# Attention with mixed heads and two MLP blocks: products with v spread over the next chunk, single banks for mixed scores, reciprocals on POOL, token weights made inside attention

## The chip, the core and the metric

The kernel runs on one core of one Trainium2 chip. The metric is the device time of one execution in microseconds. Engines: PE (TensorE: matmuls, and PEld for loading weights), DVE (VectorE), ACT (ScalarE), POOL (GpSimd) and SP, which here only issues transfers. Each engine works through its own instructions in the order in which they were written; semaphores make one wait for another.

## What is computed

```python
scores = scale * np.matmul(q, k.transpose(0, 1, 3, 2))        # B 2, H 12, S 448, D 64
scores = np.einsum('bhij,hg->bgij', scores, w_pre)            # heads are mixed
scores = scores - np.max(scores, axis=-1, keepdims=True)
attn = np.exp(scores)
attn = attn / (np.sum(attn, axis=-1, keepdims=True) + 1e-09)
attn = np.einsum('bhij,hg->bgij', attn, w_post)               # and mixed again
out = np.matmul(attn, v)
...
h = np.maximum(xt @ w_tok1, 0.0) @ w_tok2                     # token MLP over the 448 tokens
u = x + h.transpose(0, 2, 1)
h2 = np.maximum(u @ w_ch1, 0.0) @ w_ch2                       # channel MLP
return (u + h2)
...                                                           # then a gated block, GELU and a layer norm
```

The weights of the MLPs arrive as 64-bit floats and are turned into pairs of 32-bit parts (h and l) on the chip.

## The kernel before, in words

**Chunks and steps.** For each of the two batches the 448 rows of queries are cut into four chunks of 120, 120, 120 and 88 rows. A chunk is worked in steps of 20 rows; the last chunk has five, the fifth of them half as large. That makes 46 steps, numbered 0 to 45 here; chunks begin at steps 0, 6, 12, 18, 23, 29, 35 and 41.

**One step** goes through these names. `qk` (L317) makes the scores of two heads for a whole chunk on PE, into the one pair of banks `psA`, and a copy to SBUF follows (`S`, L319, on ACT; a chunk has six of these). Transfers issued by SP (L346, `P<-S`, two a step, 210 KB each) lay the scores out with the heads along the partitions, in a ring of eight tiles. `pre` (L354, PE) mixes the heads, into a pair of banks of `psB`, of which there are two. `nm` (L360, DVE) is the negative maximum, `E` (L365, ACT, two instructions) the exponential with its sum `sm`. `rc` and `rr` (L371, L373, DVE) make the reciprocal, `wt` (L377, POOL) scales the mixing weights with it. `post` (L398, PE, 64 small matmuls) mixes the heads again into the one pair of banks `psC`, and `AT` (L406, a copy on DVE, after the last `qk` on ACT) turns the result for the product with v.

**The product with v** (`av`, L421 and L427, 96 matmuls for a chunk) stands in one block behind the first step of the next chunk. It uses `psA`, the banks of `qk`. Its result is copied to `xT` by DVE and then by ACT (L433, L437).

**The order** is the order of the code: a loop over steps i, in which `pre`, `nm` and `E` work two steps ahead (LP = 2), `rc`, `rr` and `wt` one step ahead, and the transfers five steps ahead (LD = 5). Two `qk` can fall into one step. The last `qk` is in step 36.

**Behind step 36** the weights of the token MLP (four pieces, `p_t1`, `p_t2`) are fetched and converted: per piece one ACT instruction (L102), four on DVE (L120 to L126), a copy on ACT and a subtraction on DVE or POOL. `pump(4)` takes four such stages a step. In the last two steps the first batch of `xT` is turned by PE (`xps`, L446) and split (`xh` on ACT, `xl` on DVE). Then comes the last product with v, and with `t1ps` the token MLP begins; from there on the matmuls follow each other to the end.

## Time and profile before

| | us |
|---|---|
| three runs, median | 546.38 |
| three runs, lowest and highest | 544.72, 547.17 |
| the profiled execution | 544.84 |
| its span | 543.06 |
| PE busy in it | 498.2 (92%) |
| DVE busy | 353.4 (65%) |
| ACT busy | 240.8 (44%) |
| POOL busy | 157.7 (29%) |

The span runs from the first to the last instruction; 1.78 us of the execution lie outside it. A busy PE is not a PE at its peak, since matmuls overlap and their ends are modelled. In the profile two kinds of rows matter here: the chain of waits (the work that ended last, followed back from the end: start, duration, engine, tile, line) and the busy time of each engine in chosen stretches, with the granted clock of PE.

### The profile page before, as it was taken

The numbers are of one execution on the slowest core, as the hardware profiler recorded it, in microseconds if no ns is written. First come the engines' busy times: TensorE is split into PE (matmuls) and PEld (weight loads), VectorE is DVE, ScalarE is ACT, GpSimd is POOL, SyncE is SP. The second block draws the span as 40 slices with busy tenths as digits, with TensorE's granted clock in tenths as the row PEclk, the third lists the DMA queues.
The fourth block names the chain that finished last, engine by engine and source line by source line (L and its number), as shares of the span: only waits on it lengthen the run. The fifth ranks groups of instructions, "written<-read, shape, count | busy, mean of one in ns | idle before, by whom it ended". The sixth has DMA issues, their size and how long they took to land.

```text
span 543.1 us, 14017 instructions
## 1 busy us (share of the span) xinstructions
PE 498.2 (92%) x5998; PEld 408.4 (75%) x5998; DVE 353.4 (65%) x536; ACT 240.8 (44%) x454; POOL 157.7 (29%) x193
## 2 busy tenths in 40 slices
PE   7888989898897665899999999999999999999997
PEld 4345565664664553899999999999999998888986
DVE  2654657466474456295455768778887984897972
ACT  3453747467375644355333444333332344454320
POOL 2011111111021121028222322344544454057500
PEclk9989999999999775899999999999999999999999
DMA  4588435537252632031032433343353333102222
GB/s 164 178 227 233 144 95 168 156 109 212 96 179 100 183 115 64 1 118 58 1 116 98 152 120 116 113 157 100 123 168 98 100 106 123 40 1 68 88 103 102
DMA packets 25699, 63.71 MB, mean 117 GB/s; under 512 B 2836, under 2 KB 18756, under 8 KB 25636
## 3 DMA queue, kind: packets, MB, share of 16 engines
q1 hardware_dynamic: 25348, 62.42, 37.0%
q8 instruction: 47, 0.77, 0.6%
q10 hardware_dynamic: 288, 0.39, 0.2%
q14 instruction: 16, 0.13, 0.1%
HBM read 40.70 MB, written 2.75 MB: 80 GB/s over the span
## 4 chain that ended last, share of the span: by engine, by line
PE 79%; ACT 7%; DVE 6%; DMA 6%; issue 2%; SPq 0%; POOLq 0%; POOL 0%; ACTq 0%; DVEq 0%
PE post L398 6%; PE av L421 6%; PE c2ps L574 5%; PE c1ps L574 5%; PE c1ps L572 5%; PE c2ps L572 5%; PE c1ps L573 5%; PE c2ps L573 5%; PE qk L317 5%; DMA P<-S 3%; PE pre L354 3%; ACT E L365 2%; PE ups L573 2%; PE ups L572 2%; PE ups L574 2%
## 5 line engine op out<-in xcount | busy, mean ns | idle before, releaser
L147 POOL TENSOR_TENSOR wl<-cv,wh 128x768 fp32r<-128x768 f32 x28 | 52.6, 1877 | 138.8 <-ACT wh L146 104.6
L398 PEld LDWEIGHTS post<-wt,E 60*64 60x64 f32 x2880 | 54.9, 141 | 37.3 <-issue 26.8
L377 POOL TENSOR_SCALAR wt<-wd_post,rr 128x60 f32<-128x60 f32 x90 | 28.5, 332 | 168.1 <-DVE rr L373 119.6
L398 PE MATMUL post<-wt,E 60*64 60x60 f32 (+1 forms) x2880 | 55.8, 224 | 13.8 <-ACT AT L406 9.7
L365 ACT ACTIVATE E<-pre,nm 128x448 f32<-128x448 f32 x90 | 56.5, 635 | 24.8 <-DVE rc L371 18.0
L360 DVE TENSOR_REDUCE nm<-pre 128x2 f32<-128x896 f32 (+1 forms) x46 | 48.9, 1063 | 23.3 <-PE pre L354 23.3
L317 PE MATMUL qk<-kn,qn 64*64 64x448 f32 x384 | 48.3, 563 | 11.9 <-ACT xT L433 4.8
L354 PE MATMUL pre<-P,wp 64*64 64x448 f32 (+1 forms) x360 | 53.5, 557 | 5.6 <-DMA P<-S 4.1
L124 DVE SCALAR_TENSOR_TENSOR cv<-raw,cv 128x768 uint32<-128x768 uint32 (+3 forms) x44 | 54.2, 1231 | 1.4
L319 ACT COPY S<-qk 128x896 f32<-128x896 f32 x42 | 38.1, 907 | 35.4 <-PE qk L317 32.5
L574 PE MATMUL c2ps<-r1h,wl 128*128 128x448 f32 x144 | 52.6, 365 | 0.0
L573 PE MATMUL c1ps<-ul,wh 128*128 128x448 f32 x144 | 52.6, 365 | 0.0
L574 PE MATMUL c1ps<-uh,wl 128*128 128x448 f32 x144 | 52.6, 365 | 0.0
L572 PE MATMUL c2ps<-r1h,wh 128*128 128x448 f32 x144 | 52.6, 365 | 0.0
L573 PE MATMUL c2ps<-r1l,wh 128*128 128x448 f32 x144 | 52.6, 365 | 0.0
L572 PE MATMUL c1ps<-uh,wh 128*128 128x448 f32 x144 | 52.6, 365 | 0.0
L406 DVE COPY AT<-post 128x840 f32<-128x840 f32 (+1 forms) x37 | 38.9, 1052 | 16.3 <-PE post L398 15.4
L102 ACT ACTIVATE cv<-raw 128x768 f32<-128x768 f32 (+3 forms) x44 | 36.2, 824 | 23.5 <-POOL wl L147 16.7
L126 DVE SCALAR_TENSOR_TENSOR cv<-raw,cv 128x768 uint32<-128x768 uint32 (+3 forms) x44 | 40.2, 914 | 1.1
L317 PEld LDWEIGHTS qk<-kn,qn 64*64 64x64 f32 x384 | 13.8, 135 | 35.7 <-ACT S L319 14.1
L146 ACT CAST wh<-cv 128x768 fp32r<-128x768 f32 x28 | 23.4, 836 | 32.7 <-DVE cv L126 32.0
L120 DVE TENSOR_SCALAR cv<-cv 128x768 f32<-128x768 f32 (+3 forms) x44 | 30.7, 698 | 9.1 <-ACT cv L102 8.9
(188 smaller groups left out, 988.5 us busy)
## 6 DMA issues: line engine op xcount, KB each, us to landing
P<-S SPq DMA_DIRECT2D x88, 210.0 KB
raw<-in_w_ch_dram SPq DMA_DIRECT2D x24, 768.0 KB
raw<-in_w_v_dram SPq DMA_DIRECT2D x6, 512.0 KB
raw<-in_w_u_dram SPq DMA_DIRECT2D x4, 768.0 KB
raw<-in_w_out_dram SPq DMA_DIRECT2D x6, 512.0 KB
qn<-in_q_dram SPq DMA_DIRECT2D x14, 192.0 KB
vn<-in_v_dram SPq DMA_DIRECT2D x6, 448.0 KB
out_dram<-xT SPq DMA_DIRECT2D x12, 224.0 KB
```

Of the source, the lines that this page charges most:

```text
L124: nc.vector.scalar_tensor_tensor(fi, lo, 29, fi, op0=ALU.logical_shift_right, op1=ALU.bitwise_or)
L126: nc.vector.scalar_tensor_tensor(fi, hi, 0xC0000000, fi, op0=ALU.bitwise_and, op1=ALU.bitwise_or)
L147: nc.gpsimd.tensor_tensor(dst[1], f, f32(dst[0]), op=ALU.subtract)
L317: nc.tensor.matmul(ps[cols, j, :S], lhsT=qn[b, c, i // QG][rows, i % QG, h], rhs=KX[b, i][rows], start=True, stop=True)
L354: nc.tensor.matmul(ps[cols, e, :S], lhsT=wp[rs], rhs=ring[(2 * i + r) % NP_BUFS][rs], start=True, stop=True)
L360: nc.vector.tensor_reduce(out=nm[:, :ne], in_=ps[:, :ne, :S], axis=AX.X, op=ALU.max, negate=True)
L365: nc.scalar.activation(t, ps[:, e, :S], AF.Exp, bias=nm[:, e:e + 1], scale=1.0, accum_out=sm[:, e:e + 1])
L398: nc.tensor.matmul(ps[cols, r, o:o + w.stop - w.start], lhsT=E[rs, t * 64:(t + 1) * 64], rhs=wt[rs, w], start=True, stop=True)
L406: copy(dst.rearrange("p g (a i) -> p a g i", i=HB), src.rearrange("p a (g i) -> p a g i", i=HB))
L572: nc.tensor.matmul(ps, lhsT=lh, rhs=rh, start=(start and i == 0), stop=False)
L573: nc.tensor.matmul(ps, lhsT=lh, rhs=rl, start=False, stop=False)
L574: nc.tensor.matmul(ps, lhsT=ll, rhs=rh, start=False, stop=(stop and i == n - 1))
```

## The change

The change touches the attention part and the way in which the token weights are made. In words:

- The product with v of a chunk is cut into four parts (heads 0 and 1 of six pairs, 2, 3 and 4, 5), which stand in different steps of the next chunk, in a bank of their own (`psV`), each with one copy to `xT` on DVE. The last chunk's product is in two parts behind the loop, in banks of `psB`.
- `psB` becomes three single banks instead of two pairs. `nm` becomes two instructions of 448 columns instead of one of 896.
- `rc` and `rr` go from DVE to POOL, the reciprocal as a power of minus one.
- `qk` stands ahead of `pre` and at most one falls into a step, but for one step; `E` stands behind `post`; `AT` stays on DVE to step 43.
- The pieces of the token weights are fetched from step 2 on, and one stage is taken per step from step 4 to step 36, with the first operation on POOL instead of DVE; behind step 38 the first channel piece follows at one stage a step instead of four.
- The transposes of the first batch stand in steps 42 to 45, two a step.
- At the start, the mixing weights are loaded ahead of the second chunk's q, `wp` is scaled behind the first six `qk`, and the twelve first `qk` go through two pairs of banks instead of three. The first q tiles of chunk 1 are loaded twice.
- `v` of the second batch is loaded three steps later.

```diff
-        if i in p_t1:
-            nc.scalar.copy(dst[0], f)
-            yield
-            nc.vector.tensor_tensor(dst[1], f, f32(dst[0]), op=ALU.subtract)
-        elif scale is None:
-            nc.scalar.copy(dst[0], f)
+        if scale is None:
+            nc.scalar.copy(dst[0], f)
+            if early(i):
+                yield
             nc.gpsimd.tensor_tensor(dst[1], f, f32(dst[0]), op=ALU.subtract)
...
-            nc.vector.tensor_scalar(f, f, MIN_HI, MAX_HI, op0=ALU.max, op1=ALU.min)
+            (nc.gpsimd if early(i) else nc.vector).tensor_scalar(f, f, MIN_HI, MAX_HI, op0=ALU.max, op1=ALU.min)
...
-    psB = actx.enter_context(tc.tile_pool(name="psB", bufs=2, space=PSUM))
+    psB = actx.enter_context(tc.tile_pool(name="psB", bufs=3, space=PSUM))
+    psV = actx.enter_context(tc.tile_pool(name="psV", bufs=1, space=PSUM))
...
+    def b_max(i):
+        ne = steps[i][3]
+        st[i]["nm"] = ap_.tile([P, 2], F32, tag="nm", name=f"nm{i}", bufs=3)
+        for e in range(ne):
+            nc.vector.tensor_reduce(out=st[i]["nm"][:, e:e + 1], in_=st[i]["pre"][e][:, :S], axis=AX.X, op=ALU.max,
+                                    negate=True)
...
-        nc.vector.tensor_scalar(rc[:, :ne], st[i]["sm"][:, :ne], 1e-9, None, op0=ALU.add)
+        nc.gpsimd.tensor_scalar(rc[:, :ne], st[i]["sm"][:, :ne], 1e-9, None, op0=ALU.add)
         rr = ap_.tile([P, 2], F32, tag="rr", name=f"rr{i}", bufs=3)
-        nc.vector.reciprocal(rr[:, :ne], rc[:, :ne])
+        nc.gpsimd.tensor_tensor(rr[:, :ne], rc[:, :ne], mone[:, :ne], op=ALU.pow)
...
+    load_const()
     for g in range(NQ):
         load_q(0, 1, g)
-    load_const()
...
-    scale_pre()
-    both = ((psA, "A"), (psB, "B"), (psB, "B"))
+    both = ((psA, "A"), (psC, "C"))
...
+        if x == 0:
+            add(at[-1], scale_pre)
...
+        elif x + 1 < NCH:
+            for g in range(NQ):
+                add(at[0] + g, load_q, *chunks[x + 1], g)
...
-        add(first[1, 0] + 1 + g, load_v, 1, g)
+        add(first[1, 0] + 4 + g, load_v, 1, g)
...
+    add(2, w_dma)
...
+    AVS = ((0, 1), (2,), (3, 4), (5,))
+    todo = []
+    for x in range(NCH - 1):
+        f0, f1 = first[chunks[x + 1]], first[chunks[x + 2]] if x + 2 < NCH else NB
+        for hps in AVS:
+            todo.append((f0 + hps[0] * (f1 - f0) // NP, *chunks[x], hps))
+
+    def next_av(i):
+        while todo and todo[0][0] <= i:
+            _, b, c, hps = todo.pop(0)
+            av(b, c, hps, nc.vector.tensor_copy)
+
+    def next_turn(i, n):
+        if i + LD > NB and turns:
+            ps = one(psV, "V", f"xps0_{len(turns)}") if n else pair(psA, "A", f"xps0_{len(turns)}")[:, 0]
+            turn(ps, *turns.pop(0))
...
     for i in range(-LD, NB):
         for fn, a in extra.get(i, []):
             fn(*a)
-        if 0 <= i + LP < NB:
+        ahead = 0 <= i + LP < NB
+        due = list(scores.get(i, []))
+        if due:
+            qk(*due.pop(0))
+        if ahead:
             b_pre(i + LP)
-        due = scores.get(i, [])
-        if due:
-            qk(*due[0])
-        if 0 <= i + LP < NB:
-            b_exp(i + LP)
+        next_turn(i, 0)
+        if ahead:
+            b_max(i + LP)
         if 0 <= i + 1 < NB:
             b_norm(i + 1)
+        for d in due:
+            qk(*d)
         if i >= 0:
+            next_av(i)
             b_post(i)
-            for d in due[1:]:
-                qk(*d)
-            b_turn(i, nc.vector.tensor_copy if i <= LAST else nc.scalar.copy)
-            if i in starts and i:
-                av(*chunks[chunks.index(steps[i][:2]) - 1])
+        if ahead:
+            b_exp(i + LP)
+        if i >= 0:
+            b_turn(i, nc.vector.tensor_copy if ahead else nc.scalar.copy)
+        next_turn(i, 1)
         if i + LD < NB:
             b_dma(i + LD)
...
-        if i > LAST + 2:
-            pump(4)
+        if 4 <= i <= LAST or i > LAST + 2:
+            pump(1)
...
-    av(*chunks[-1])
+    for x, copy in enumerate((nc.vector.tensor_copy, nc.scalar.copy)):
+        hps = range(x * (NP // 2), (x + 1) * (NP // 2))
+        av(*chunks[-1], hps, copy, (psB, "B"))
```

PE around the product with v of chunk 1 (`av_1`), before: steps 12 and 13 (`post` ends step 12).

```order
L398 MATMUL post_1101<-wt_0_1034,E_0_964 64x60 x12
L398 MATMUL post_1101<-wt_0_1034,E_0_964 64x30 x4
L398 MATMUL post_1101<-wt_1_1036,E_1_966 64x60 x12
L398 MATMUL post_1101<-wt_1_1036,E_1_966 64x30 x4
L421 MATMUL av_1_1135<-AT_1_663,vn_0_316 64x120 x12
L421 MATMUL av_1_1135<-AT_1_663,vn_1_374 64x120 x12
L421 MATMUL av_1_1135<-AT_1_663,vn_2_447 64x120 x12
L427 MATMUL av_1_1135<-AT_1_663,vn_0_316 64x120 x4
L427 MATMUL av_1_1135<-AT_1_663,vn_1_374 64x120 x4
L427 MATMUL av_1_1135<-AT_1_663,vn_2_447 64x120 x4
L354 MATMUL pre_1188<-P_100,wp 64x448 x2
L354 MATMUL pre_1188<-P_101,wp 64x448 x2
```

PE in the changed kernel, step 15 of the same chunk, with two of the six pairs of heads of chunk 1.

```order
L329 MATMUL qk_0_2_1365<-kn_1_599,qn_0_0_819 64x448 x4
L370 MATMUL pre_0_1371<-P_101,wp 64x448
L370 MATMUL pre_1_1372<-P_101,wp 64x448
L370 MATMUL pre_0_1371<-P_102,wp 64x448
L370 MATMUL pre_1_1372<-P_102,wp 64x448
L443 MATMUL av_1_3_1388<-AT_1_709,vn_1_394 64x120 x6
L443 MATMUL av_1_3_1388<-AT_1_709,vn_2_465 64x120 x6
L449 MATMUL av_1_3_1388<-AT_1_709,vn_0_332 64x120 x2
L449 MATMUL av_1_3_1388<-AT_1_709,vn_1_394 64x120 x2
L419 MATMUL post_1406<-wt_0_1301,E_0_1271 64x60 x12
L419 MATMUL post_1406<-wt_0_1301,E_0_1271 64x30 x4
```

The block of 96 matmuls has become four groups of 32 or 16, each between `pre` and `post` of a step, and `qk` has moved ahead of `pre`.

ACT behind the last `qk` before, steps 37 to 39: `E` and `AT` take turns, and from step 39 the conversion of weights (L102) follows.

```order
L365 ACTIVATE E_0_2907,sm_2906<-pre_2899,nm_2904 128x448
L365 ACTIVATE E_1_2909,sm_2906<-pre_2899,nm_2904 128x448
L406 COPY AT_2_2742<-post_2919 128x4x42x5
L365 ACTIVATE E_0_2965,sm_2964<-pre_2957,nm_2962 128x448
L365 ACTIVATE E_1_2967,sm_2964<-pre_2957,nm_2962 128x448
L406 COPY AT_2_2742<-post_2977 128x4x42x5
L365 ACTIVATE E_0_3023,sm_3022<-pre_3015,nm_3020 128x448
L365 ACTIVATE E_1_3025,sm_3022<-pre_3015,nm_3020 128x448
L406 COPY AT_2_2742<-post_3035 128x4x42x5
L102 ACTIVATE cv_3073<-raw_2955 112x512
```

DVE in the changed kernel in steps 37 and 38: `AT` stands here, behind the two `nm` and the copy of a part of the product with v.

```order
L376 TENSOR_REDUCE nm_3022<-pre_0_3016 128x1
L376 TENSOR_REDUCE nm_3022<-pre_1_3017 128x1
L456 COPY xT<-av_1_2_3033 128x12x10
L427 COPY AT_2_2906<-post_3043 128x4x42x5
L376 TENSOR_REDUCE nm_3092<-pre_0_3086 128x1
L376 TENSOR_REDUCE nm_3092<-pre_1_3087 128x1
L456 COPY xT<-av_1_3_3103 128x2x12x10
L427 COPY AT_2_2906<-post_3121 128x4x42x5
```

In these steps ACT has kept only `E`, and `AT` has moved to DVE; the first operation on the token weights, which followed in step 39, is not among them.

## Rows read from the trace of the kernel before

**Rows 1.** Busy time by stretch: us, then each engine (instructions), granted clock, DMA share, GB/s.

```profile
0.00:25.33 25.33, 20.46 (x202) 9.39 (x204) 10.39 (x15) 9.56 (x16) 4.12 (x14) 1.00 0.52 170
25.33:56.55 31.22, 26.74 (x649) 16.80 (x647) 17.27 (x30) 15.05 (x36) 4.81 (x16) 0.95 0.78 216
56.55:169.03 112.48, 101.16 (x2776) 66.87 (x2777) 70.33 (x123) 66.20 (x152) 17.60 (x59) 1.00 0.45 139
169.03:224.66 55.63, 35.33 (x812) 27.27 (x805) 28.46 (x56) 27.71 (x60) 8.15 (x17) 0.72 0.38 113
224.66:543.06 318.40, 314.49 (x1566) 288.09 (x1566) 226.99 (x313) 122.26 (x195) 123.00 (x87) 1.00 0.30 97
```

**Rows 2.** Chain of waits, steps without product with v: start, us, what.

```profile
153.30 0.78 PE pre L354 x8
154.08 0.75 PE qk L317 x8
154.83 0.91 PE post L398 x64
```

**Rows 3.** Chain of waits at a product with v, and the turning copy of step 36.

```profile
160.74 3.84 PE av L421 x72
164.58 0.82 PE av L427 x24
165.42 0.80 DVE xT L433
166.24 0.79 ACT xT L433
...
169.03 1.07 DVE AT L406
```

**Rows 4.** Chain of waits in a step with two score products.

```profile
150.56 0.81 ACT S L319
151.41 0.98 PE qk L317 x8
```

**Rows 5.** Chain of waits behind step 36.

```profile
181.15 1.00 DVE nm L360
182.24 1.34 ACT E L365 x4
183.58 0.90 ACT AT L406
184.61 1.93 PE post L398 x64
...
208.85 0.57 DVE xl L450
```

**Rows 6.** Busy time by stretch, two short ones, columns as in the first group.

```profile
132.00:136.00 4.00, 2.54 (x70) 1.34 (x62) 2.36 (x4) 2.15 (x5) 0.60 (x2) 1.00 0.67 225
180.00:184.00 4.00, 1.28 (x27) 0.37 (x19) 2.94 (x6) 1.76 (x5) 0.89 (x2) 0.91 0.83 213
```

**Rows 7.** DVE by line and shape: count, busy us, mean ns, idle before.

```profile
L406 DVE COPY AT<-post 128x840 f32<-128x840 f32 x36 | 38.3, 1065 | 16.3 <-PE post L398 15.4
L433 DVE COPY xT<-av 128x360 f32<-128x360 f32 x6 | 4.7, 791 | 22.0 <-PE av L427 22.0
L124 DVE SCALAR_TENSOR_TENSOR cv<-raw,cv 128x768 uint32<-128x768 uint32 x28 | 40.2, 1435 | 0.9
```

**Rows 8.** Instructions of one tile, ns as least/median/most: two of POOL.

```profile
L377 POOL TENSOR_SCALAR wt<-wd_post,rr x90: 310/317/907, 23.7 to 204.0; 128x60 f32<-128x60 f32 x90
L748 POOL TENSOR_TENSOR rq<-rs,mhalf x7: 549/552/562, 473.5 to 492.3; 128x1 f32<-128x1 f32 x7
```

**Rows 9.** Timeline: the start's scaling, a maximum of one bank, a slow conversion.

```profile
9.05 0.20 DVE L70 TENSOR_SCALAR wp<-wd_pre 128x64 f32<-128x64 f32 x1 [8.05 <-DMA wd_pre<-in_w_pre_dram]
105.40 0.62 DVE L360 TENSOR_REDUCE nm<-pre 128x1 f32<-128x448 f32 x1 [0.78 <-PE pre L354]
203.00 1.25 DVE L122 TENSOR_SCALAR cv<-cv 128x448 uint32<-128x448 uint32 x1
```

More of the change, by code (lines that the diff above doesn't have):

```diff
@@ L126, in w_conv @@
             nc.vector.scalar_tensor_tensor(fi, hi, 0xC0000000, fi, op0=ALU.bitwise_and, op1=ALU.bitwise_or)
-            w_abs(i + 1)
+            if not early(i):
+                w_abs(i + 1)
         yield
-        if p_t2[0] <= i <= p_c1[1]:
+        if i in p_c1[:2]:
             yield
@@ L153, in conv_steps @@
         for i in range(len(pieces)):
+            while i not in wstate["raw"]:
+                yield
             for _ in w_conv(i):
@@ L158, in conv_steps @@
             yield
+            if early(i + 1):
+                yield
     def pump(n):
@@ L346, in b_dma, with one @@
             nc.sync.dma_start(out=ring[(2 * i + r) % NP_BUFS][PAD:PAD + ne * HW], in_=src)
+    def one(pool, tag, nm):
+        return pool.tile([P, 512], F32, tag=tag, name=nm)
     def b_pre(i):
         ne = steps[i][3]
-        ps = st[i]["pre"] = pair(psB, "B", f"pre{i}")
+        ps = st[i]["pre"] = [one(psB, "B", f"pre{i}_{e}") for e in range(ne)]
         for r, cols in enumerate(HALVES):
@@ L407, in b_turn, with av @@
         st[i] = None
-    def av(b, c):
+    def av(b, c, hps, copy, pool=None):
         s0, n = CH[c]
@@ L413, in av @@
         cols = IB * (nb + (rest > 0))
-        ps = pair(psA, "A", f"av{b}_{c}")
+        ps = one(*(pool or (psV, "V")), f"av{b}_{c}_{hps[0]}")
         at = AT[b, c]
-        for hp in range(NP):
-            x, o = hp % 2, hp // 2 * cols
+        for m, hp in enumerate(hps):
+            o = slice(m * cols, (m + 1) * cols)
             for s in range(NK // 2):
                 for j, out_rows in enumerate(HALVES):
-                    w = vn[b, hp // 2][:, ((x * 2 + j) * (NK // 2) + s) * D:][:, :D]
-                    nc.tensor.matmul(ps[out_rows, x, o:o + cols], lhsT=w,
-                                     rhs=at[:, s * H + x * (H // 2) + hp // 2 * 2 + j, :cols],
-                                     start=(s == 0 and hp < 2), stop=False, skip_group_check=True)
@@ L424, in av @@
-        for hp in range(NP):
-            x, o = hp % 2, hp // 2 * cols
+                    w = vn[b, hp // 2][:, ((hp % 2 * 2 + j) * (NK // 2) + s) * D:][:, :D]
+                    nc.tensor.matmul(ps[out_rows, o], lhsT=w, rhs=at[:, s * H + 2 * hp + j, :cols],
+                                     start=(s == 0 and m == 0), stop=False, skip_group_check=True)
+        for m, hp in enumerate(hps):
+            o = slice(m * cols, (m + 1) * cols)
+            x, g = hp // (NP // 2), hp % (NP // 2)
@@ L431, in av @@
[L431 to L438 removed]
+        t0 = s0 + b * S
@@ L553, in tile_kernel @@
             RX[0] = [t[:, NS * C:NS * C + TOK // P * C].rearrange("p (t c) -> p t c", c=C) for t in XR]
-        if i + LP >= NB:
-            for _ in range(2):
-                ps = pair(psB, "B", f"xps0_{len(turns)}")
-                for j in range(2):
-                    turn(ps[:, j], *turns.pop(0))
-    av(*chunks[-1])
+    while turns:
+        turn(one(psB, "B", f"xps0_{len(turns)}"), *turns.pop(0))
+    for x, copy in enumerate((nc.vector.tensor_copy, nc.scalar.copy)):
+        hps = range(x * (NP // 2), (x + 1) * (NP // 2))
+        av(*chunks[-1], hps, copy, (psB, "B"))
     actx.close()
@@ L643, in tile_kernel @@
         tok2(1)
-    tctx.close()
-    wvp = ctx.enter_context(tc.tile_pool(name="wv", bufs=1, reuse_waits="tile"))
-    for j in V_EARLY.values():
-        wvt[j] = [wvp.tile([P, 1, DH], F32R, name=f"wv{j}{nm}") for nm in "hl"]
+    for n, j in enumerate(V_EARLY.values()):
+        wvt[j] = [shared[:, 2 * n + m].unsqueeze(1) for m in range(2)]
     wstate["bar"] = p_v[NCC - 2]
```

120 lines of the change are left out of this document (63 added, 57 removed).

## The prediction, made before the changed kernel ran

> **What bounds the kernel now.** I read the busy time by stretch first. Behind 224.66 us, where the token MLP begins, PE is busy for 314.49 of 318.40 us at a granted clock of 1.00: that stage is PE's, and the change leaves its matmuls as they are. What can move lies before it [rows 1], in four stretches: the start to 25.33; steps 0 to 6 to 56.55, where the transfers are densest (DMA share 0.78); steps 7 to 35 to 169.03; and the tail, steps 36 to 45, where PE is busy for 35 of 55.6 us at a mean clock of 0.72.
>
> Then the chain of waits, to see what an ordinary step needs. Without a product with v it is PE alone: `pre` 0.78, `qk` 0.75, `post` 0.91, together 2.44 us [rows 2]. A product with v adds 3.84 + 0.82 = 4.66 us of PE, 0.78 for each of six pairs of heads, and behind it stand the two copies to `xT`, 0.80 and 0.79, since the next `qk` wants the same bank [rows 3]. In a step with two `qk` the second waits for the copy `S` of the first, 0.81, which is queued on ACT behind `E` [rows 4]. In the tail the chain goes round four engines: `nm` 1.00, `E` 1.34, `AT` on ACT 0.90, `post` 1.93. That last is twice the 0.91 of before: the lower of PE's two levels, 1.2 instead of 2.4 GHz [rows 2, 5].
>
> **The change part by part**, against the profiled execution (544.8 us: span 543.06 and 1.78 outside; the median is 1.5 higher).
>
> *Start, to 25.33: 0.* The twelve first `qk` lose a third bank pair. At worst each then takes about 1.0 instead of 0.75 us, as the second of two in a step did [rows 2, 4]: 12 x 0.25 = 3 us lost. `wp` no longer holds DVE until its weights land at 9.05 [rows 9], which can give 1 us. Transfers set most of this stretch (PE is busy for 20.5 of 25.3), so I take nothing, with -3 to +1 as ends.
>
> *Steps 0 to 6: 3 us.* The product with v here shrinks from six pairs to two (4 x 0.78 = 3.1 us; the other four move on into the next stretch), and with it go the copies, 1.6. Against that the token weights now arrive here too. The DMA share of 0.78 speaks for transfers setting the pace, PE's 26.74 of 31.22 for PE [rows 1]. I take 3, with 0 (transfers alone) and 5 as ends.
>
> *Steps 7 to 35: 13 us.* PE's need is 29 x 2.44, less 0.85 for one half-sized step, plus four products with v of 4.66 and a narrower one of about 3.5: 92 us. The stretch lasts 112.5, so 20.5 are waits. Of these, five times the copies to `xT` are 5 x 1.59 = 8.0: they go, since a bank of its own holds each part until DVE copies it, two to three steps ahead of the next part. Six steps have two `qk`; I put the second one's wait at 1.5 each, an estimate from `S` 0.81 and about half of an `E` ahead of it [rows 4, 5], together 9; after the change one such step is left. The rest, 3.5, is around the loads of v (from 132 to 136 PE is busy for 2.54 of 4 us at a DMA share of 0.67 [rows 6]) and between steps. Moving v three steps later shifts it and does not remove it. What can be late next is DVE: per step two `nm` of 0.62 (a pair together took 1.00, so 0.24 is added), `AT` 1.07, about 0.33 for `xT` (an estimate: 1.59 over six steps, and a start more), and one stage of a conversion, at 512 columns two thirds of 1.43 [rows 5, 7, 9]: 2.6 without a conversion, up to 3.6 in one step of six with the dearest stage, 2.9 to 3.2 as I count the mixture. The stretch now takes 112.5/29 = 3.9 a step, PE alone would take 92/29 = 3.17. So DVE stands just below PE. I take 13 of the 17; ends 4 (the waits move to DVE and the transfers) and 19.
>
> *Reciprocals on POOL: 0.* The trace has no reciprocal of two columns on POOL. Its nearest row is a power of one column, 0.55; `wt` takes 0.32 [rows 8]. With an addition like `wt`, the chain `rc`, `rr`, `wt`, `wt` is 0.32 + 0.55 + 2 x 0.32 = 1.5 us, 2.1 if two columns cost double. Ends: none if it fits into a step of 3.2 (it is wanted one step later, and `E` is what it waits for), 0.5 a step if queued behind a conversion's stage on POOL. I take none, by the rows named; DVE loses two small instructions a step.
>
> On where this belongs the Trainium skill speaks against the change: GPSIMD Engine Reference, § 4.1 Engine selection, puts ordinary elementwise work on VectorE and calls GpSimd about twice as slow with two inputs. For so small a tile the rows show fixed costs; by the page's factor the same chain is still shorter than a step.
>
> *Tail, 169.03 to 224.66: 18 us.* The change takes the token weights off this stretch, puts `AT` on DVE, and `E` behind `post`, so ACT has `E` alone. DVE then has 13 `nm` of 0.62 (8.1), seven `AT` of 1.07 (7.5), copies to `xT` of some 3.1, the operations of one channel piece, about 4 with the dearest at 1.43, and eight `xl` of 0.57 (4.6) [rows 5, 7, 9]: 27.3 us. To that come about six waits of DVE for a `post`, roughly one each, and the last product with v, 3.5 at 90 columns: 37 to 37.5 instead of 55.6, a gain of 18. PE needs less at full clock (ten steps of `pre` and `post`, 1.69, and 16 pairs of heads, 12.4 at most: 29 us). At the low level that would double, and PE, not DVE, would set the pace: it would be busy without a break, which in the stretch from 180 to 184, where it was busy for 1.28 of 4 us before falling to the low level, it was not [rows 6]. Ends: 9 (half clock stays) and 21.
>
> *Behind 224.66: 0.* The first channel piece starts a step later at a slower rate, covered by the token MLP; its cost without cover is its four DVE operations, about 4 us. The copies `xT` ahead of the MLP are in the tail's sum.
>
> Sum: 0 + 3 + 13 + 0 + 18 + 0 = 34. 544.8 - 34 = **511 us**.
>
> **The rivals.**
>
> *Transfers pace the body.* Each step's `P<-S` and the loads share the queue of SP, and the weights add to it. For: a DMA share of 0.78 in the first steps, and PE at 2.54 of 4 us around the v loads. Against: 0.45 on average in steps 7 to 35 [rows 1, 6]. The gain there falls to 4, that of steps 0 to 6 to 0: 34 - 12 = 22, 523 us.
>
> *DVE or the clock holds the tail.* The rounds `nm`, `E`, `post`, `AT` still run over three engines, and PE stays at the low level. For: 0.72 there, 1.93 for a `post`. Against: two fewer operations of others on ACT and DVE in the round [rows 1, 5]. The gain of 18 becomes 9: 520 us.
>
> *Reciprocals on POOL come late.* `post` waits 0.5 us a step, 46 x 0.5 = 23: 534 us. For: on POOL a `wt` took up to 0.91 [rows 8], and a DVE conversion beside POOL's work took 1.25 us [rows 9]; now POOL has a conversion's stage too. Against: the result has a step to arrive.
>
> *All three at once*: no gain worth naming, about 543 us.
>
> *The slower one: half clock in the body.* Six banks in turn (`psA`, `psB`, `psV`, `psC`) put a short wait between each two groups of matmuls; if PE falls to its low level for it, a step costs 2.44 + 0.78 = 3.2 us more. 34 / 3.2: from 11 of 46 steps on the gain is gone; with 20 steps it is 511 + 64 = 575 us. For: the tail's 0.72 with PE busy for 64% of it. Against: the body is at 1.00 although its waits now are longer and as many [rows 1, 6].
>
> The Trainium skill has a rule that would lead there: TensorE: Matmul & The Clock Gate, § A second HAM failure mode: psum-queue depth-cycling, where a kernel that cycled through PSUM banks left PE idle for short moments and its clock went to and fro. The body's granted clock, 1.00, shows no such thing before the change.
>
> **How the numbers follow.** The forecast, 511 (its own range 503 to 519, from the smaller ends of the stretches): 0.59. Transfers, 523: 0.17. Tail, 520: 0.12. Late reciprocals, 534: 0.05. All three, 543: 0.03. Half clock, 575: 0.04. A measurement of this kernel can tell about 0.5% (2.7 us) from no change. Faster 0.93, same 0.03 (the case of all three), slower 0.04. The range 502 to 526 takes in the first three with their ends and leaves out the last three and a little of the first ones' edges.
>
> **What would show each step right or wrong.** Right: between steps 7 and 35 no row of PE waiting for a copy to `xT`, a step near 3.4 us, a clock of 1.00, and `t1ps` at about 190 us. The tail, from the `AT` of step 36 on, near 38 us with DVE busy for 70% or more. Wrong: `post` waiting for `wt` or POOL in the chain (reciprocals); `pre` waiting for `P<-S` in more steps than those around the v loads (transfers); a clock under 0.9 in the body; DVE at over 95% there, with `pre` waiting for `nm` or `E` to free one of the three single banks; or `t1ps` starting early and the MLPs lasting longer than 318 us because channel weights are late.

## The result

The changed kernel takes 526.86 us (median, 525.68 to 528.32) where the kernel before took 546.04 beside it: a ratio of 0.9651, interval 0.9617 to 0.9684, faster by 3.5%. The prediction was 511, range 502 to 526. The sign was right; the gain, 19 us, is a little over half of the 34 forecast, and the time lies 0.9 us above the range. The profiled execution took 526.59, 1.79 of it outside a span of 524.80.

Busy time by stretch in the changed kernel, cut at the same events as [rows 1] (the copies `AT` of steps 0, 7 and 36, and the start of `t1ps`); columns as there.

```profile
0.00:25.64 25.64, 21.56 (x202) 9.09 (x202) 10.19 (x14) 9.81 (x16) 6.42 (x21) 1.00 0.60 190
25.64:51.75 26.11, 22.31 (x592) 13.11 (x590) 15.97 (x25) 14.88 (x36) 12.93 (x30) 1.00 0.85 247
51.75:161.77 110.02, 103.82 (x2774) 70.81 (x2766) 76.20 (x123) 67.91 (x152) 56.72 (x124) 1.00 0.54 160
161.77:205.20 43.43, 37.17 (x876) 26.38 (x874) 25.85 (x43) 17.12 (x43) 14.65 (x32) 0.92 0.42 120
205.20:524.80 319.60, 315.74 (x1569) 287.95 (x1566) 225.30 (x312) 121.35 (x195) 120.90 (x86) 1.00 0.30 94
```

| stretch | before | after | gain | forecast |
|---|---|---|---|---|
| start to step 0 | 25.33 | 25.64 | -0.3 | 0 (-3 to 1) |
| steps 0 to 6 | 31.22 | 26.11 | 5.1 | 3 (0 to 5) |
| steps 7 to 35 | 112.48 | 110.02 | 2.5 | 13 (4 to 19) |
| tail | 55.63 | 43.43 | 12.2 | 18 (9 to 21) |
| MLPs | 318.40 | 319.60 | -1.2 | 0 |

So two steps of the sum are to be explained: 10.5 us missing from the body (steps 7 to 35), and 6 from the tail. The chain of waits (start, duration, engine, tile, line) shows the first. In steps that wait for no transfer it is PE alone, without the waits of [rows 3] and [rows 4], and still hardly shorter. Step 16 has no part of a product with v, step 17 has one pair of heads, step 18 two.

```profile
85.11 0.78 PE qk L329 x6
85.89 0.73 PE pre L370 x7
86.62 0.89 PE post L419 x54
87.55 0.78 PE qk L329 x7
88.33 0.93 PE pre L370 x8
89.26 0.77 PE av L443 x12
90.03 0.21 PE av L449
...
91.28 0.78 PE qk L329 x6
92.07 0.75 PE pre L370 x8
92.82 1.38 PE av L443 x24
94.20 0.45 PE av L449 x5
```

From `qk` to `qk` that is 2.44 us without a part, 3.73 with one pair and 4.38 with two. The forecast had priced a pair at 0.78, by the block of [rows 3].

Over the whole stretch the chain before had 74.2 us of PE, 7.0 of copies to `xT`, 7.5 of `S`, 8.1 of `E` and 5.7 of transfers. After the change the copies are gone and 1.8 of `S` and 0.8 of `E` are left, but the chain has 90.8 us of PE and 14.0 of transfers, counted from issue to landing.

The tail's chain shows the second. The last `P<-S` lands 11.3 us after its issue; `xl` waits for it, and the maxima are queued on DVE behind `xl`.

```profile
172.84 11.29 DMA P<-S
...
184.45 0.56 DVE xl L473
185.00 1.06 DVE nm L376 x2
```

### The profile page after: what moved, and what is told of

It reads as the page before. It is cut to its first block, busy times and chain, and to the rows that moved or that the text cites. A ratio compares the mean times of both kernels' runs of the same rounds, so it can differ in the third digit from the quotient of the medians.

```text
span 524.8 us, 14033 instructions
## 1 busy us (share of the span) xinstructions
PE 500.6 (95%) x5998; PEld 407.3 (78%) x5998; DVE 353.5 (67%) x513; ACT 231.1 (44%) x439; POOL 211.6 (40%) x292
## 4 chain that ended last, share of the span: by engine, by line
PE 82%; DMA 8%; DVE 3%; issue 2%; ACT 2%; POOL 1%; SPq 1%; POOLq 0%; DVEq 0%; ACTq 0%
PE pre L370 6%; PE post L419 6%; PE c2ps L622 6%; PE c1ps L623 6%; PE c1ps L622 6%; PE c2ps L623 6%; PE c1ps L621 6%; PE c2ps L621 6%; PE qk L329 5%; PE av L443 5%; DMA P<-S 5%; DMA qn<-in_q_dram 2%; PE vps L621 2%; PE vps L623 2%; PE ups L621 2%
## 5 line engine op out<-in xcount | busy, mean ns | idle before, releaser
L376 DVE TENSOR_REDUCE nm<-pre 128x1 f32<-128x448 f32 x90 | 52.0, 619 | 25.8 <-PE pre L370 25.6
L419 PE MATMUL post<-wt,E 60*64 60x60 f32 (+1 forms) x2880 | 59.3, 219 | 4.9 <-issue 3.9
L370 PE MATMUL pre<-P,wp 64*64 64x448 f32 (+1 forms) x360 | 55.6, 550 | 3.8 <-DMA P<-S 2.3
L427 DVE COPY AT<-post 128x840 f32<-128x840 f32 (+1 forms) x44 | 46.3, 1052 | 15.5 <-PE post L419 15.4
L136 DVE SCALAR_TENSOR_TENSOR cv<-raw,cv 128x768 uint32<-128x768 uint32 (+3 forms) x44 | 53.1, 1208 | 1.1
L392 POOL TENSOR_SCALAR rc<-sm 128x2 f32<-128x2 f32 (+1 forms) x46 | 11.8, 258 | 95.4 <-ACT E L385 95.4
L443 PEld LDWEIGHTS av<-AT,vn 128*64 128x64 f32 x576 | 28.9, 140 | 20.3 <-issue 10.4
L138 DVE SCALAR_TENSOR_TENSOR cv<-raw,cv 128x768 uint32<-128x768 uint32 (+3 forms) x44 | 40.2, 915 | 1.1
L370 PEld LDWEIGHTS pre<-P,wp 64*64 64x64 f32 (+1 forms) x360 | 20.6, 133 | 24.2 <-issue 10.4
L154 ACT CAST wh<-cv 128x768 fp32r<-128x768 f32 x28 | 23.4, 836 | 31.6 <-DVE cv L138 31.0
```

The source lines that it names most:

```text
L136: nc.vector.scalar_tensor_tensor(fi, lo, 29, fi, op0=ALU.logical_shift_right, op1=ALU.bitwise_or)
L370: nc.tensor.matmul(ps[e][cols, :S], lhsT=wp[rs], rhs=ring[(2 * i + r) % NP_BUFS][rs], start=True, stop=True)
L376: nc.vector.tensor_reduce(out=st[i]["nm"][:, e:e + 1], in_=st[i]["pre"][e][:, :S], axis=AX.X, op=ALU.max, negate=True)
L419: nc.tensor.matmul(ps[cols, r, o:o + w.stop - w.start], lhsT=E[rs, t * 64:(t + 1) * 64], rhs=wt[rs, w], start=True, stop=True)
L427: copy(dst.rearrange("p g (a i) -> p a g i", i=HB), src.rearrange("p a (g i) -> p a g i", i=HB))
L443: nc.tensor.matmul(ps[out_rows, o], lhsT=w, rhs=at[:, s * H + 2 * hp + j, :cols], start=(s == 0 and m == 0), stop=False, skip_group_check= ...
```

## Experiments

Beside each measured time stands its ratio to the kernel before, run beside it on the same chip. The table gives where each profiled execution stood (us from the start of its span); "body" is from the `AT` of step 7 to that of step 36, "tail" from there to `t1ps`.

| kernel | AT of step 7 | body | tail | span |
|---|---|---|---|---|
| before | 56.55 | 112.48 | 55.63 | 543.06 |
| changed | 51.75 | 110.02 | 43.43 | 524.80 |
| e1, two parts | 54.16 | 115.90 | 42.7 | 531.5 |
| e2, six parts | 54.26 | 113.04 | 45.0 | 531.7 |
| e3, reciprocal on DVE | 53.31 | 111.17 | 43.2 | 526.5 |
| e4, channel loads late | 53.03 | 110.90 | 40.7 | 523.8 |
| e5, token weights late | 49.93 | 111.01 | 48.0 | 528.2 |
| e7, q once | 52.84 | 108.71 | 41.4 | 522.4 |
| e10, channel loads split | 54.27 | 106.54 | 38.0 | 518.4 |
| e11, without loads of k and v | 53.39 | 105.13 | 41.4 | 519.0 |
| e12, as e13, two parts | 55.64 | 107.26 | 36.8 | 519.1 |
| e13, split and q once | 53.54 | 108.63 | 37.7 | 519.6 |
| e14, as e13, v early | 53.85 | 110.58 | 37.7 | 521.7 |
| e17, bank by bank | 52.96 | 107.65 | 43.5 | 523.1 |
| e18, split, bank by bank | 53.42 | 108.80 | 38.3 | 519.7 |

### How many parts: e1 and e2

```diff
-    AVS = ((0, 1), (2,), (3, 4), (5,))
+    AVS = ((0, 1, 2), (3, 4, 5))                     # e1
+    AVS = ((0,), (1,), (2,), (3,), (4,), (5,))       # e2
```

> The changed kernel with the product with v in two parts of three pairs of heads instead of four. Theory (parts): each part costs PE a fixed 0.64 us, whatever its size: in the trace of the changed kernel a step without a part takes 2.44 us, one with one pair 3.73, one with two pairs 4.38, so the first pair of a part costs 1.29 and the second 0.65. Two parts less in each of seven chunks save 14 x 0.64 = 9.0 us: 518 us, and 519 to 521 where transfers hold some of the steps. A step with three pairs should take 2.44 + 0.64 + 3 x 0.65 = 5.0 us. Rival (transfers or DVE pace steps 7 to 35): no change, 526 to 528.

> The changed kernel with the product with v in six parts of one pair each. Theory (parts): two parts more in each of seven chunks, 14 x 0.64 = 9.0 us, 536 us (some of it hidden beside transfers: 532 to 536). Rival (transfers or DVE pace the steps): 526 to 529.

Measured: e1 532.28 us (0.9772, 0.9732 to 0.9812), e2 533.24 (0.9796, 0.9752 to 0.9840). Six parts came out where the theory had them, but two parts did not gain, they lost. Where no transfer holds a step, from the `AT` of step 12 to that of step 27, the changed kernel took 52.89 us, e1 52.68, e2 54.93: the direction is the theory's, but of the 0.64 us a part, 0.04 is left for the five parts that e1 has less there, and 0.34 for the six that e2 has more (which hold one narrow pair more, too). A part of three pairs in the chain of e1:

```profile
102.47 0.75 PE pre L370 x4
103.22 2.00 PE av L443 x36
105.22 0.45 PE av L449 x6
```

The 36 matmuls take 2.00 us, 56 ns each; in a part of one pair they took 64, in one of two 57, in the block of [rows 3] 53. A step with three pairs takes 5.2 us in e1, one with one pair 3.55 in e2: a further pair costs 0.82, and the fixed price of a part is nearer 0.3 than 0.64. What made e1 slower is not its parts: its first part wants more of v at once, and step 29 took 12.70 us there (6.37 in the changed kernel), 4.0 of them in a wait for v.

```profile
PE av L443 <- DMA vn<-in_v_dram: 4.0, 1, 4.0
```

That is the list of waits of PE in e1 (total, times, longest). So the number of parts alone, two or four, is not the cause of the missing 10 us.

### The remainder's order: e9

The kernel before, with one line changed (the second loop over pairs, L424).

```diff
-        for hp in range(NP):
+        for hp in (0, 2, 4, 1, 3, 5):
             x, o = hp % 2, hp // 2 * cols
```

> The kernel before, with the 24 remainder matmuls of each product with v (L427, 64 rows) ordered so that the pairs of heads of the upper rows come first and those of the lower rows behind them; before, pair by pair, upper and lower rows take turns. Theory (a price of the parts): before, the 24 take 0.82 us (34 ns each) because neighbours use different rows of the array and run side by side; in the changed kernel, where a part has one bank and one half of the rows, eight take 0.45 us (56 ns each). Half by half, L427 takes about 24 x 0.057 = 1.4 us a chunk, 8 x 0.55 = 4 to 5 us more in all: 549 us where before is 544.7. Rival: the order is free, L427 stays at 0.82 and the time at 544 to 546.

Measured: 545.82 us, ratio 1.0019 (0.9976 to 1.0062): no difference that can be told. In the trace a step with a product takes about 0.25 us more (8.48 for 8.24, 8.48 for 8.18, 8.04 for 7.79, 7.07 for 6.89), half of what was expected, 2 us in all if it all counted; in step 13 it took 10.15 for 8.26, since PE had stood still for 2.0 us ahead of it for nothing that the profile shows and went on at a granted clock of 0.72 from 72 to 78 us. In the changed kernel the 24 remainder matmuls of a chunk cost 1.47 us on the chain (L449, 7.9% of 18.55 us, shown below at e17), 0.65 more than the block's 0.82, so the order explains 0.25 of that and the rest is open. Each part there has one bank and one half of the rows. The Trainium skill (TensorEngine Tiling (Array Packing), § Gotcha 1: PSUM Pressure) says that different row tiles cannot access one PSUM bank at the same time; no run here shows it, since a part with both halves of the rows in its bank was not tried.

### The product with v left out: e15 and e16

```diff
     def next_av(i):                                  # e15; e16 drops the call in the loop of before
         while todo and todo[0][0] <= i:
             _, b, c, hps = todo.pop(0)
-            av(b, c, hps, nc.vector.tensor_copy)
+            pass
```

> The changed kernel without the products with v of the first seven chunks (their matmuls and copies are left out and xT is filled with zeros, so the time measures the rest). Theory: PE sets the body, and a chunk's product costs 5.8 to 6.2 us of PE in four parts, against 4.66 in one: a chunk of six steps without waits for transfers (21.2 us in the changed kernel) takes 15.0 to 15.4 us, 2.5 to 2.56 a step; where the forecast's price held it would be 16.5. Rival (ACT or DVE sets a plain step at 2.6 to 2.7): 15.6 to 16.2 us, and the product's price on the path is 5.0 to 5.6. Transfers then hold more steps, since they have less cover.

> The kernel before without the products with v of the first seven chunks (left out as in the other run). Theory: a chunk's product cost 4.66 of PE and 0.8 to 1.6 of waits for the copies to xT on the path, 5.5 to 6.2 a chunk, which is what the four parts cost too, and so the body gained little: the step with the product (8.2 us) takes 2.4 to 2.7 without it, and a chunk of six steps 16.3 (five of 2.44 and one of 4.05 with two score products) where it took 22.15. Rival (the copies to xT were hidden): the difference is 4.7 us a chunk.

Measured: 508.63 and 515.47 us, once each, beside 546.59 for the kernel before. Their totals say little, since without the products more steps wait for transfers; the clean steps, those that wait for no transfer, say much. The length of a step is read from the start of its `AT` and of the one ahead. First the two ends of step 13, before and in e16, then those of steps 16 to 21 in the changed kernel and of steps 35 to 40 in e15:

```profile
71.68 1.07 DVE L406 COPY AT<-post 128x840 f32<-128x840 f32 x1
79.94 1.07 DVE L406 COPY AT<-post 128x840 f32<-128x840 f32 x1 [1.39 <-PE post L398]
```

```profile
68.47 1.07 DVE L406 COPY AT<-post 128x840 f32<-128x840 f32 x1
71.16 1.07 DVE L406 COPY AT<-post 128x840 f32<-128x840 f32 x1 [0.31 <-PE post L398]
```

```profile
85.17 1.07 DVE L427 COPY AT<-post 128x840 f32<-128x840 f32 x1 [0.33 <-PE post L419]
...
106.35 1.06 DVE L427 COPY AT<-post 128x840 f32<-128x840 f32 x1
```

```profile
142.82 1.06 DVE L427 COPY AT<-post 128x840 f32<-128x840 f32 x1
...
158.53 1.05 DVE L427 COPY AT<-post 128x840 f32<-128x840 f32 x1
```

- Before: the steps with a product, 8.26, 8.18, 7.79 and 8.24 us (steps 13, 19, 30, 36), take 2.69, 2.44, 2.39 and 2.98 without it. A chunk's product cost 5.5 us on the path, the mean of the four.
- Changed: six steps with a whole chunk's product (16 to 21) take 21.18 us; six without (35 to 40 of e15) take 15.71, about 2.61 each; the last four of them have no `qk`, but steps with one take 2.61 too (16, 34, 36). A chunk's product costs 5.5 us on the path.

The same. So it is with the same six steps on both sides, waits for transfers and stops of PE included: 21.18 and 16.95 (steps 16 to 21, changed and e15), 22.15 and 18.34 (steps 31 to 36, before and e16), 4.2 and 3.8 us. The change took the waits for `xT` (some 0.8 us a chunk beside PE's 4.66, less than the 1.59 of the copies) out of the product, and the product paid them back as PE time by standing in four parts. And a plain step of e15 takes 2.61 where before it took 2.44, also behind step 36, where there is no `qk`. The waits of PE's weight loads from 148 to 158 us of e15 (total, times, longest) show what holds it there:

```profile
PEld pre L370 <- ACT E L385: 2.9, 4, 0.7
```

In the kernel before two pairs of banks let `pre` run ahead; with three single ones `pre` of a step waits for `E` of the step before to give a bank back. For e15 the rival's numbers came true (15.6 to 16.2, 5.0 to 5.6). For e16 the theory's price of a product did (5.5), but not its chunk: 18.34 us for the 16.3 expected, 1.5 of them in stops of PE for nothing that the profile shows.

### The round through three banks: e17 and e18

```diff
-        for r, cols in enumerate(HALVES):
-            for e in range(ne):
+        for e in range(ne):
+            for r, cols in enumerate(HALVES):        # in b_pre; e18 has e10's edit too
```

> The changed kernel with the eight matmuls of pre ordered bank by bank (first bank complete, then the second) instead of alternating. Theory (the round through three banks): pre's first bank is free from the step before and its maximum starts 0.35 to 0.4 us earlier, pre waits for E only for its second bank; a plain step falls from 2.61 to 2.70 us to about 2.45 to 2.5, some 29 x 0.15 to 0.2 = 4 to 6 us in the body and 1 to 2 in the tail: 519 to 522. Rival (DVE or ACT is full in a plain step): no change, 525 to 528. Rival (the matmuls of one bank don't run beside each other, so pre takes 1.1 instead of 0.75 us): 46 x 0.35 = 16 us more, 540 to 544.

> The same order of pre, with the second and third load of channel weights behind steps 41 and 42. Theory: the two gains add up, 520.7 less 4 to 7: 514 to 517, about what the prediction had for the change (511). Rival (both shorten the same wait of the tail, or the transfers take the body's gain): 518 to 521.

Measured: e17 524.27 us (0.9615, 0.9556 to 0.9673), e18 520.70 (0.9562, 0.9502 to 0.9621). From step 12 to step 27 e17 took 52.48 us, the changed kernel 52.89. The five steps without a part became 0.05 to 0.11 us shorter, the others stayed as they were; the theory had 0.15 to 0.2 in every step. e18 came out where its rival had it. So the round of `pre`, `nm` and `E` through three banks sets a step where the product is left out; with the product it costs that little, and PE sets the rest. What PE does in the body of the changed kernel, by line of its chain from 85.05 to 103.6 (18.55 us, five steps, six pairs):

```profile
by line: PE post L419 25.0%; PE av L443 23.1%; PE qk L329 22.8%; PE pre L370 21.1%; PE av L449 7.9%
```

The two `av` lines are 31.0% of 18.55, 5.75 us for six pairs, against 4.66; the rest is 2.56 a step, against 2.44. Both make a chunk 1.8 us dearer on PE. The 2.56 is a mean: step 16, without a part, takes 2.44 as before, and beside its part a step takes 2.5, or 2.7 where it follows a step without one. There `pre` takes 0.93 instead of 0.75, whatever comes behind it, as e1's chain shows between two plain steps:

```profile
110.11 0.93 PE pre L370 x8
111.03 0.47 PE post L419 x28
```

In e2, where each step has its part, `pre` nearly always takes 0.75. In e17 the same `pre` takes 0.85 (step 17), so part of it is the round through three banks. What the parts themselves do to PE, by their change between 128 and 64 rows, their one bank or their order, no run separates.

### Transfers in the body: e7, e11 and e14

```diff
-        elif x + 1 < NCH:                            # e7: chunk 1's q loaded once
+        elif 0 < x < NCH - 1:
...
     def load_v(b, g):                                # e11, and load_k alike
+        if b:
+            vn[b, g] = vn[0, g]
+            return
...
-        add(first[1, 0] + 4 + g, load_v, 1, g)       # e14, with e7's and e10's edits
+        add(first[1, 0] + 4 + g // 2 * 2, load_v, 1, g)
```

> The changed kernel without the second load of chunk 1's q (576 KB less on the transfers at the start). Theory (transfers set the first 52 us, DMA share 0.85 in steps 0 to 6): the seventh AT comes 1 to 2 us earlier than the 51.8 to 54.3 of the runs so far, 524.5 to 526 in all. Rival (PE sets them): no change, 526 to 527.5.

> The changed kernel without the loads of k and v of the second batch (the first batch's are used again: part of the input is left out, so its time is only a measure of these loads): four loads in steps 4 to 7, three in steps 27 to 29. Theory (transfers hold some steps of the body): the steps that took over 4.4 us without a second score product lose their excess. Steps 28 and 29 together take about 7 instead of 10.75 us, and steps 5, 6, 8 and 9 together about 15 instead of 21.2: 8 to 10 us less, 517 to 519. Rival (PE or DVE sets the body, and the transfers only take its slack): 525 to 527.

> The same with v of the second batch loaded in steps 27, 27 and 29 instead of 27, 28 and 29, so that what the first part needs in step 29 is asked for a step earlier. Theory: the wait of step 29 for v (1.8 us in the changed kernel) goes: 1 to 2 us less than without this edit, 517 to 519. Rival: the transfers are full there, and what v gains P<-S loses: no change, 518 to 521.

Measured (the second load of q is two transfers of 192 KB, so 384 KB, not the 576 that e7's text gives): e7 523.96 us (0.9609, 0.9549 to 0.9668), e11 521.09 (0.9555, 0.9493 to 0.9618), e14 523.16 (0.9594, 0.9531 to 0.9657).

In e11 steps 28 and 29 take 3.34 and 4.34 us where the changed kernel has 4.38 and 6.37; the changed kernel's chain waits there for v:

```profile
126.60 8.72 DMA vn<-in_v_dram
```

Steps 8 and 9 take 3.50 and 4.37 for 3.86 and 6.21. The body is 105.1 us for 110.0. So transfers do hold the body, for 5 us in this pair of executions, and for 1.4 against e10, which has these loads and a body of 106.5. The expected gain in steps 5 and 6 did not come (6.65 and 5.86 us for 5.47 and 5.71): there the chain waits for `P<-S` with or without the loads of k. e7's theory fell as well: step 7 came at 52.84, not earlier, and its smaller time comes from body and tail, which its edit does not touch. e14 moved a wait from step 29 (6.28 in e13, 5.63) to step 28 (3.31, 5.98): v and `P<-S` come through the same queue, and e14's rival was right.

How the waits of the first 52 us and of steps 28 and 29 fall differs between executions by some us: step 7 came between 51.75 and 54.27 in kernels that are the same up to there (changed, e4, e10), and the body took 106.5 to 110.9 in kernels whose body is the same (the same three).

### The tail: e4, e10 and e5

The second and third of the loads of channel weights, 768 KB each, move behind the last `P<-S`, in e4 the first too.

```diff
-        if 0 < i - LAST <= RB:
+        if 0 < i - LAST - 3 <= RB:                   # e4
+        if i - LAST in (1, 5, 6):                    # e10
             w_dma()
```

> The changed kernel with the first three loads of channel weights issued behind steps 40 to 42 instead of 37 to 39, behind the last P<-S. Theory (tail): those loads of 768 KB made the last P<-S land only at 184.1 us, 11.3 us after their issue; xl, which overwrites the tile that they read, stood in DVE's queue for it for 3.0 us, with the maxima behind it, and PE fell to half clock behind that. The wait goes and the tail shortens by 3 to 6 us: 521 to 524, if the weights that come later are still hidden. Rival (the tail is the rounds of nm, E, wt, post): no change, 526 to 528. Rival (late channel weights hold the MLP): the token MLP begins earlier but the time is 527 or more.

> The changed kernel with the first load of channel weights issued behind step 37, as it was, and the second and third behind steps 41 and 42 instead of 38 and 39, so that only one stands ahead of the last P<-S. Theory (tail): neither the wait of xl for the last P<-S nor that of the conversion for its weights is left, and the stretch from the AT of step 36 to t1ps takes 38 to 40 us, where the changed kernel took 43.4 and the run with all three late 40.7: 522 to 524. Rival: the tail is bound by its rounds, 43 us, 526 to 528; or the later pieces hold the channel MLP, and the stretch behind t1ps is longer than 319.6 by what the tail gains.

Measured: e4 525.23 us (0.9660, 0.9626 to 0.9694), e10 520.74 (0.9564, 0.9489 to 0.9639). e4's tail is 2.7 us shorter, and a new wait of ACT stands in it (total, times, longest), for the first piece itself, with `E` queued behind it:

```profile
ACT cv L114 <- DMA raw<-in_w_ch_dram: 5.6, 1, 5.6
```

e10 has no wait of `xl` for `P<-S`, and 0.6 us for the first piece. Its tail takes 38.0 us at the higher level of the clock; the changed kernel's fell to the lower one behind the wait. First the changed kernel, then e10 (whole tail in the last row):

```profile
182.00:186.00 4.00, 1.88 (x80) 1.61 (x76) 1.55 (x4) 0.74 (x2) 0.00 (x0) 1.00 0.07 26
186.00:190.00 4.00, 3.61 (x14) 1.52 (x16) 2.67 (x5) 1.62 (x6) 2.48 (x4) 0.51 0.00 0
190.00:194.00 4.00, 4.00 (x96) 3.70 (x94) 1.68 (x3) 1.03 (x3) 1.12 (x3) 0.63 0.03 6
```

```profile
182.00:186.00 4.00, 4.00 (x100) 2.91 (x92) 3.27 (x6) 0.96 (x2) 1.54 (x4) 1.00 0.01 4
186.00:190.00 4.00, 3.52 (x148) 3.11 (x144) 3.32 (x5) 2.41 (x5) 1.13 (x3) 1.00 0.03 6
190.00:194.00 4.00, 2.95 (x67) 2.15 (x58) 2.01 (x5) 1.87 (x4) 0.00 (x0) 1.00 0.62 201
...
160.81:198.80 37.99, 33.87 (x877) 24.66 (x875) 25.95 (x43) 17.15 (x43) 13.96 (x32) 1.00 0.47 137
```

The granted clock (the third number from the end of a row) is 0.51 from 186 to 190, the level of 1.2 GHz, after PE had been idle for more than half of the 4 us ahead. The stretch behind `t1ps` is 319.6 us in both, so the later channel weights cost nothing there. The tail's gain is not that of one execution: with the second and third load late the tail took 36.8 to 38.3 us in five kernels (e10, e12, e13, e14, e18), and 41.4 to 45.0 in the seven that have the changed kernel's order of loads there and the products (changed, e1, e2, e3, e7, e11, e17). In total e10's median lies 6 us under that of the changed kernel, though the intervals of their ratios overlap.

```diff
-        return i <= p_t2[-1]
+        return False                                 # e5: token weights as before
...
-        if 4 <= i <= LAST or i > LAST + 2:
-            pump(1)
+        if i > LAST + 2:
+            pump(4)
```

> The changed kernel with the token weights made behind step 36, as in the kernel before (same ring of raw tiles, four stages a step, the first operation on DVE); everything else as changed. Theory (the tail's gain is the early weights): the tail takes 50 to 56 us instead of 43.4, as before (55.6), and the body, without the 2 MB of these loads and their operations, is 1 to 4 us shorter: 531 to 538. Rival (the transfers pace the body, and the early weights cost there what they give): within 2 us of the changed kernel, 525 to 529.

Measured: 528.13 us (0.9660, 0.9570 to 0.9750). The tail takes 48.0 us, 4.6 more than in the changed kernel and 2 short of the expected; 1.8 come back at the start, where step 7 comes at 49.93. In total it cannot be told from the changed kernel, as the rival had it. So the early weights are worth some 5 us in the tail of the changed kernel, and 10 against e10, whose chain has no wait for `P<-S` there, as e5's has none. The rest of the tail's gain (55.6 to 48.0) is left to `AT` on DVE, `E` behind `post`, the parts and the earlier transposes, which no run took apart.

### The reciprocal back on DVE: e3

```diff
-        nc.gpsimd.tensor_tensor(rr[:, :ne], rc[:, :ne], mone[:, :ne], op=ALU.pow)
+        nc.vector.reciprocal(rr[:, :ne], rc[:, :ne])          # and the addition for rc
```

> The changed kernel with the addition and the reciprocal back on DVE (as an addition and a reciprocal, L392 and L394). Theory: POOL's chain is hidden in the body and costs the tail a little, since there each step waits for E, then rc 0.23, rr 0.71, wt 0.61: the time stays within 1 us, 526 to 528, or falls by 1 to 2 in the tail. Rival (late reciprocals hold post): about 0.5 us a step less, 504 to 510. Rival (DVE is the bound): 46 steps x about 0.3 us more, 535 to 540.

Measured: 528.42 us (0.9718, 0.9687 to 0.9749). From step 12 to step 27 it took 53.27 us for 52.89, 0.03 a step; neither rival came near. In total it is a little slower than the changed kernel, and not within the 1 us of the theory: the ratios, 0.9718 (0.9687 to 0.9749) and 0.9651 (0.9617 to 0.9684), lie apart. On POOL `rr` took 0.71 us, on DVE 0.17; the rows are groups by line of the changed kernel, and the chain of e3:

```profile
L394 POOL TENSOR_TENSOR rr<-rc,mone 128x2 f32<-128x2 f32 (+1 forms) x27 | 19.2, 712 | 2.2
```

```profile
191.41 0.17 DVE rr L394
```

That is a factor of four, but between two different operations, a power and a reciprocal; the same addition (`rc`) took 0.23 on POOL and 0.16 on DVE. The rule of the Trainium skill that the prediction weighed (GPSIMD Engine Reference, § 4.1 Engine selection) has a factor of about two for elementwise work with two inputs; no run here has one such operation on both engines. The slower reciprocal cost nothing in the body, where the result is wanted a step later. In the tail `rc`, `rr` and `wt` stand on the chain of the changed kernel with 2.8 us, but what that costs does not show: the tail took 43.2 us with the reciprocal on DVE, 4.5 of them in a stop of PE described below, and 43.4 on POOL.

### All together: e12 and e13

e13 has the edits of e7 and e10; e12 also e1's two parts, with v of the second batch in steps 26, 26 and 27.

> The changed kernel with the later channel loads (behind steps 37, 41 and 42) and without the second load of chunk 1's q. Theory: the two gains add up, 520.7 less 1 to 2.5: 518 to 520. Rival: the gain of the single q load was another course of the same transfers and not of its own: 520 to 522.

> The changed kernel with the later channel loads (behind steps 37, 41 and 42), without the second load of chunk 1's q, and with two parts of three pairs of heads, for which v of the second batch is loaded in steps 26, 26 and 27. Theory: a part costs some 0.35 us beside its pairs (one part of six pairs 4.66, two 5.4, four 5.75 to 6.1, six 6.2), so two parts less in a chunk give 0.4 to 0.7 us, 3 to 5 in all, against the same kernel with four parts, where the v loads don't hold step 29: 515 to 518. Rival (a plain step is then bound by ACT and DVE, 2.6 to 2.7 us, and takes it back): the same as with four parts, 518 to 521.

Measured: e13 520.57 us (0.9558, 0.9482 to 0.9634), e12 520.47 (0.9568, 0.9503 to 0.9634), e10 alone 520.74. Neither the single load of q nor two parts add anything that can be told. In both the rival was right.

## Why the prediction was right and wrong

**Start, 0: right.** -0.3, and from -1.3 to 0.5 in e4 and e10, which are the same up to there. Fewer bank pairs and the freed DVE balanced, or neither counted.

**Steps 0 to 6, 3: right.** 5.1 in the profiled execution; counted together with the start, 2.3 to 4.8 by where step 7 came in the kernels that are the same up to there. The mechanism was the forecast's: step 7, which has no block of a product ahead of it any more, took 2.65 us for 7.79, and steps 1 to 6 took 23.4 in both. In those the DMA share is 0.85 before and after, and the chain of the changed kernel waits for `P<-S`, 3.0 and 5.7 us: there the transfers set the pace.

**Steps 7 to 35, 13: the step that failed.** It is the term "five times the copies to `xT` are 5 x 1.59 = 8.0: they go, since a bank of its own holds each part". The waits went, but two things in it were wrong. On the path they had been worth 0.8 us a chunk and not 1.59 (e16), and the forecast kept the price of a pair at 0.78, the price of the block, for parts of one and two pairs. In these parts six pairs cost 5.75 us of PE instead of 4.66, and on the path a chunk's product costs 5.5 before and after (e15, e16). That term was worth nothing. Why PE takes longer for the parts stays open. The other large term, the steps with two `qk`, was right: 4.05 us such a step took, 2.44 a plain one, 1.6 each for six steps, one of which remains, so 8.0. (The 17 of waits that the forecast drew on counts all six; with one left it is 15.5.) Against it stands the rest of a step, which is dearer, 2.56 on PE for 2.44, where the forecast left it as it was. On clean steps a chunk of six fell from 22.15 us (steps 31 to 36 before) to 21.18, 4.7 us for 29 steps: the 8.0 less some 3.3 for the dearer rest, an estimate. The profiled execution kept 2.5 of them, others 1.6 to 5.9; the waits for transfers in steps 8, 9, 11, 28, 29 and 33 are most of the difference. The prediction's first rival, a gain of 4 here because transfers pace the body, had nearly the number, with the lesser half of the cause.

DVE, which the prediction took for the next one late, was not: it was busy for 76.2 of 110.0 us, and 0.6 us of the chain are its.

**Reciprocals, 0: right.** The chain is 0.23 + 0.71 + 0.60 = 1.5 us, the forecast's figure, and e3 shows that it is covered in the body.

**Tail, 18: short by 6, one thing left out.** The 37 to 37.5 us of the sum are there, 38.0, once the second and third load of channel weights do not stand ahead of the last `P<-S` (e10). That they agree so well is in part luck: DVE's work was sized about right (25.95 us for 27.3), but it does not set the pace, as the sum had it. Of e10's 38 us the chain has 24.6 on PE, 4.6 on ACT, 3.4 on DVE and 2.9 on POOL. What was left out is that the transposes moved to step 42, two steps earlier, and that `xl` writes the tile from which the last `P<-S` read. The prediction had looked at what the moved instructions cost, and not at what their output overwrites. Its rival for the tail had the lower clock staying; it came behind that wait, for some 7 of the 8 us from 186 to 194.

**MLPs, 0:** -1.2, without a cause that a run shows.

**The slower rival** did not come: the body's clock stayed at 1.00 with PE's banks split into six tiles in turn instead of four, and the rule of the Trainium skill named there (TensorE: Matmul & The Clock Gate, § A second HAM failure mode: psum-queue depth-cycling) did not act in this kernel.

Of the rivals' own sums one does not add up: all three at once would take 12, 9 and 23 us off a gain of 34, which gives 555 us and not 543. It changes nothing here.

**Still open:** in the tail of e1, e2 and e3 PE stood still in the middle of `post` for 4.2, 4.1 and 4.5 us, for nothing that the profile shows, while transfers were dense:

```profile
176.60 4.48 issue
```

This is the chain of e3; the DMA share from 175 to 180 was 0.86. e10 has such a stop of 1.8, the kernel before one of 1.5. The page of the profile lists a DMA queue of instructions (q8), and in e1 and e3 one transfer of it falls into the stop; whether it was late is not settled.

## What to carry to other kernels

A product that is cut up to fill gaps has its price taken from small pieces, not from the block: here a step became up to 1.3 us longer by a part of one pair, in the block a pair took 0.78, and the cut gave back what the removed wait had been worth. When instructions move earlier, look at which transfers still read the tile that they write, and what else is in those transfers' way: two loads of 768 KB, issued three steps later, were worth about as much in the tail (5.4 us) as making four weight pieces early was in the changed kernel (4.6). Test the cost of work on the path by leaving it out on both sides of a change; busy time had shown the product before at 4.66, the chain with its copies at 6.25, and on the path it was worth 5.5.

## What the runs showed of the hardware

- A group of `av` matmuls over all 128 rows, between groups of 64 rows, took 64 ns a matmul with 12 of them, 57 with 24, 56 with 36 and 53 with 72 (time on the chain by their number).
- Remainder matmuls whose neighbours use the other half of the rows took 34 ns each (24 in 0.82 us, before), in one bank and one half some 60 ns (12 in 0.70 us, e1); put half by half into two banks they made a step only about 0.25 us longer for 24 (e9).
- The last `P<-S`, issued behind three loads of 768 KB, landed after 11.3 us; with one such load ahead of it (e10) nothing waited for it.
